# Block-causal attention and a SoLU layer on one core: squares to a scratch tile, spaced source rows, one copy for the second AV result, new planner constants

## The chip, the cores and the metric

The kernel runs on one core of a Trainium2 chip. A core has TensorE (PE, matmuls, with its weight loads shown apart as PEld), VectorE (DVE), ScalarE (ACT), GpSimd (POOL), SyncE (SP, which here issues the DMAs) and 16 DMA engines. The metric is device time in microseconds of one execution, lower is better. The kernel before took 726.27 us, the median of 3 runs (724.88 to 729.66).

## The reference

Attention over 8 batches of 8 heads, 576 positions, head width 64, in float32, with a causal mask in blocks of 64 positions, and then a layer on the 4608 tokens of width 512 with an inner width of 1024:

```python
scores = scale * np.matmul(q, k.transpose(0, 1, 3, 2))
mask = block_i >= block_j
scores = np.where(mask, scores, -1000000000.0)
scores = scores - np.max(scores, axis=-1, keepdims=True)
attn = np.exp(scores)
attn = attn / (np.sum(attn, axis=-1, keepdims=True) + 1e-09)
# np.matmul(attn, v), then heads side by side: x is [4608, 512]
h = x @ w_in                                   # w_in float64
e = np.exp(h - h.max(-1)); sm = e / (e.sum(-1) + 1e-9)
solu = h * sm
ln = (solu - mean) / np.sqrt(var + 1e-06) * g_ln
out = (ln @ w_out).astype(np.float32)
```

The weights come as float64; the kernel reads their 32-bit words and builds float32 values from them.

## The kernel before, in words

**Attention.** Two heads of a batch are one pair, 32 pairs in all. Queries are cut into units of 128 rows, `(h, i)` for head h and block i, 0 to 3; a unit needs 128·(i+1) keys. The last 64 queries of both heads form one unit, `LAST`. For each pair, PE makes the scores (L567, L573), DVE masks and takes the row maxima (L598, L602), ACT does the exponentials and their sums (L614), and the rows are divided by their sums on POOL, DVE or ACT (L632 to L634). The probabilities lie in `pb`, four rows of 25 slots of 32 columns in each partition; `soff` gives each unit's first slot. They must be transposed before the AV product. For the first eight entries (`PEP`, the four pairs of batch 0 in two parts each), PE transposes them (L554). For the other 28, DVE transposes blocks of 32 by 32 (L640), and four DMAs from SP (`place`, L648) carry 32 partitions of `pb` each to 128 partitions of `pt`. The AV product (L660) multiplies `pt` with the values in `vr` into two PSUM banks: `av0` takes the queries up to 384, `av1` the other 192 of each head. ACT or DVE copies both to the tile `xt` (`copy`, L412): `av0` in one piece, `av1` in three, since its two halves hold their columns in a different order.

**The layer.** A tile is 128 tokens, 36 in all, of three batches' `xt` in rotation. Matrices are split in a high and a low part, so each product is three matmuls. PE makes `h` (L746, two halves of 12 matmuls of 512 columns; the second product, L816, has as many), DVE takes the maximum (L752), ACT the exponential (L753), DVE the product (L754), POOL centres it (L761). ACT squares it and sums the squares (L764): only the sum `m[:, 4:5]` is used, the squared values go to the output tile `ob[i]`, `i = t % 2`, and are overwritten later. DVE transposes blocks (L782) and four DMAs move them (`ct` from `zb`, L786), the result is split (L794 to L798), PE makes the second product (L816), ACT or DVE writes it, scaled, to `ob[i]` (L820, L821), and SP stores it (L822). The first four tiles and the last use PE for the transpose (L804).

**The start.** The first batch's `q`, `k` and two blocks of `v` are fetched first (`fetch0`, L435, L438); then `prep` (L362 to L380) turns each of 8 blocks of `w_in` and 8 of `w_out` into high and low parts on ACT, POOL and DVE.

**The order of the work.** Nothing is ordered at run time. `Schedule.run` simulates the five engines when the kernel is built: each operation has a duration, a key, and perhaps alternatives on other engines; when an engine is free, it takes the ready operation with the smallest key, and the order found is written out. DMA operations carry `dma`, the time that they occupy the queue, and `tail`, the time from there to landing; SP is held back when the queue is more than `DEPTH` ahead. Keys are built from the dictionary `PARAMS`: attention's are the pair's number p plus a constant by kind (`s` scores, `se` maxima and exponentials, `sr` and `sp` division, `pt` transposes, `pe` placing, `av` and `ae` AV product and copies, `ld` and `lv` loads; an ending `32` for the first eight entries, `A` for the first part of batch 0), the layer's are `h0` (first four tiles: `hA`) plus `hs` per tile, and the weights' are `w0 + w1·n` for `w_in` and `w2 + w3·c` for `w_out`. Engines work through their queues in order.

The lines that write `ob` and place the probabilities:

```python
ACT.activation(ob[i].bitcast(mybir.dt.bfloat16), cz, AF.Square, accum_out=m[:, 4:5])   # L764
for a_ in (0, 2, 1, 3):                                                              # L647, L648
    SP.dma_start(pt_[:, a_].rearrange("p s i -> p (s i)"), pb[32 * a_ : 32 * a_ + 32].rearrange("p r s i -> p (r s i)"))
```

Of the kernel before, what the change touches and what calls it, by code (L numbers as in the profile page):

```python
# [31 lines left out]
NPT = 2  # L32
# [15 lines left out]
    "a_sp": 15.151, "a_sp32": 33.434, "a_lf": -19.843, "a_w": -53.076, "a_xh": 7.699, "a_xl": 42.171,  # L48
    "a_c": 45.045, "a_o": 1.147, "np": 32, "l0": 10.919, "a_cl": 82.304, "a_ai": -19.611, "aff": -198.558,
    "a_t3": -226.025, "a_cm": -13.873, "a_cg": -136.828, "a_sa": -14.146, "a_sa32": 226.312, "a_qh": -1.948,  # L50
    "a_kl": -33.0, "a_ch": 8.609, "a_chd": 185.089, "a_clo": -87.939, "ct0": -0.422, "qA": -20.741,
    "qeA": -57.386, "sA": -4.436, "seA": -5.607, "srA": 89.822, "spA": 243.774, "ptA": 46.328, "peA": -58.037,
    "avA": 18.17, "aeA": 50.13, "ldA": -276.676, "lvA": 10.694, "a_spA": -0.83, "a_saA": 1.199, "w2": 5.397,
    "w3": 49.83, "hA": 84.857,
# [7 lines left out]
class Schedule:  # L62
# [49 lines left out]
    def run(self):  # L112
# [20 lines left out]
        while events:  # L133
# [18 lines left out]
            for e in engs:  # L152
# [59 lines left out]
def kernel(  # L212
# [73 lines left out]
    ms = [sb(f"ms{i}", [8]) for i in range(2)]  # L286
# [22 lines left out]
    def PS(i):  # L309
        return pst[sc.slot[i]]  # L310
# [73 lines left out]
    n = 0  # L384
# [490 lines left out]
```

## Time and profile before

| | |
|---|---|
| time, median of 3 | 726.27 us (724.88 to 729.66) |
| profiled execution, its own time | 728.37 us |
| its span, first to last instruction | 726.6 us |
| mean granted TensorE clock | 0.974 |
| moved by DMA | 109.74 MB, mean 151 GB/s |

The page gives one profiled execution. An engine's busy time is a share of the span; "idle before" names the time an engine stood still just before a group of instructions, and what ended it. A line such as `PE ps L660 <- DMA pt<-pb: 4.1, 4, 1.2` says that PE stood before instructions of line 660 until a DMA from `pb` to `pt` landed, 4.1 us in total, 4 times, 1.2 us at most. In a table of stretches, each row has the stretch, its length, the busy time of each engine with its instructions, the granted clock of PE, the mean busy share of the DMA engines and the GB/s moved. A line of the timeline has start, duration, engine, line, operation and count, and in brackets the idle time before it with its cause.

### The profile page before, as it was taken

What the parts mean: (1) busy time and instruction counts of PE and PEld (TensorE: products, weight loads), DVE (VectorE), ACT (ScalarE), POOL (GpSimd) and SP (SyncE); (2) the same over time, 40 slices, a digit from 0 to 9 for tenths busy, and PEclk for the clock granted to TensorE, in tenths of its full rate; (3) what the DMA queues carried; (4) which work ended last, traced back from release to release, by engine and by line L of the source; (5) the groups of instructions that cost most, each with busy time, mean ns of one, the idle gap of its engine ahead of it and who ended that gap; (6) DMA issues with size and microseconds to landing.
All of it is one profiled execution on the core that took longest, in us unless ns stands there. A gap on an engine that the chain in (4) does not pass through costs nothing.

```text
span 726.6 us, 14364 instructions
## 1 busy us (share of the span) xinstructions
PE 673.5 (93%) x4747; PEld 530.2 (73%) x4747; DVE 574.3 (79%) x1252; ACT 499.8 (69%) x1286; POOL 359.6 (49%) x512
## 2 busy tenths in 40 slices
PE   5687897999999999989999999999989999999997
PEld 4565575777777777767777777777767777788885
DVE  2798989896999888978798979698878977455552
ACT  3686889686878867767786778587857885444432
POOL 1367566443665454546555554556456555223211
PEclk8598989999999999999999999999999999999999
DMA  9855358596969897969896989797969767322221
GB/s 172 195 96 130 99 114 141 123 130 169 165 170 174 213 176 194 155 166 172 203 172 163 176 205 158 173 187 180 179 160 188 171 167 168 105 72 72 73 73 44
DMA packets 223434, 109.74 MB, mean 151 GB/s; under 512 B 186496, under 2 KB 202368, under 8 KB 223360
## 3 DMA queue, kind: packets, MB, share of 16 engines
q1 hardware_dynamic: 222320, 108.56, 74.9%
q8 instruction: 37, 0.61, 0.4%
q10 hardware_dynamic: 1040, 0.26, 0.2%
q14 instruction: 37, 0.30, 0.1%
HBM read 37.23 MB, written 9.44 MB: 64 GB/s over the span
## 4 chain that ended last, share of the span: by engine, by line
PE 55%; DVE 12%; DMA 12%; ACT 9%; SPq 6%; issue 3%; POOL 2%; DVEq 0%; ACTq 0%; POOLq 0%
PE ps L816 20%; PE ps L746 16%; PE ps L660 9%; PE ps L573 6%; DMA pt<-pb 5%; ACT pb L614 3%; PE ps L567 3%; DVE nm L602 2%; DMA kz<-in_k_dram 2%; SPq L648 2%; DVE pb L640 2%; ACT pb L634 2%; DMA ct<-zb 2%; SPq L461 2%; DMA ub<-in_moe_w_in_dram 1%
## 5 line engine op out<-in xcount | busy, mean ns | idle before, releaser
L614 ACT ACTIVATE pb<-ps,nm 128x384 f32<-128x384 f32 (+4 forms) x288 | 157.1, 555 | 74.2 <-DVE nm L602 58.6
L602 DVE TENSOR_REDUCE nm<-ps 128x1 f32<-128x384 f32 (+4 forms) x288 | 132.1, 505 | 0.4
L640 DVE STREAM_TRANSPOSE pb<-pb 128x1536 f32<-128x1536 f32 (+1 forms) x56 | 101.6, 1829 | 11.4 <-ACT pb L634 7.8
L660 PE MATMUL ps<-pt,vr 128*64 128x128 f32 (+1 forms) x1648 | 92.6, 269 | 12.9 <-DMA ct<-zb 7.1
L660 PEld LDWEIGHTS ps<-pt,vr 128*64 128x64 f32 x1648 | 81.8, 137 | 30.8 <-issue 12.7
L634 ACT ACTIVATE pb<-pb,rz 128x512 f32<-128x512 f32 (+4 forms) x185 | 92.1, 566 | 17.4 <-DVE rz L625 14.5
L746 PE MATMUL ps<-wih,xh 128*128 128x512 f32 x288 | 84.3, 414 | 3.7 <-ACT pb L614 3.7
L798 POOL TENSOR_TENSOR cl<-ct,ch 128x512 fp32r<-128x512 f32 x40 | 51.6, 1293 | 71.0 <-ACT ch L794 69.0
L632 POOL TENSOR_SCALAR pb<-pb,rz 128x512 f32<-128x512 f32 (+4 forms) x101 | 63.9, 644 | 40.3 <-DVE rz L625 17.1
L816 PE MATMUL ps<-woh,ch 128*128 128x512 f32 x288 | 80.7, 402 | 0.0
L746 PE MATMUL ps<-wil,xh 128*128 128x512 f32 x288 | 79.5, 398 | 0.0
L816 PE MATMUL ps<-woh,cl 128*128 128x512 f32 x288 | 78.8, 395 | 0.0
L746 PE MATMUL ps<-wih,xl 128*128 128x512 f32 x288 | 78.7, 395 | 0.0
L816 PE MATMUL ps<-wol,ch 128*128 128x512 f32 x288 | 78.7, 395 | 0.0
L761 POOL TENSOR_SCALAR ub<-ub,ms 128x1024 f32<-128x1024 f32 x31 | 35.7, 1151 | 82.7 <-DVE ms L755 68.5
L573 PE MATMUL ps<-kh,qh 64*128 64x128 f32 (+3 forms) x256 | 58.3, 386 | 11.4 <-ACT pb L614 7.5
L746 PEld LDWEIGHTS ps<-wih,xh 128*128 128x128 f32 x288 | 50.9, 190 | 23.8 <-issue 8.6
L746 PEld LDWEIGHTS ps<-wil,xh 128*128 128x128 f32 x288 | 54.8, 190 | 13.0
L746 PEld LDWEIGHTS ps<-wih,xl 128*128 128x128 f32 x288 | 54.3, 189 | 13.1 <-POOL xl L725 0.3
L816 PEld LDWEIGHTS ps<-woh,cl 128*128 128x128 f32 x288 | 54.2, 188 | 12.8
L816 PEld LDWEIGHTS ps<-wol,ch 128*128 128x128 f32 x288 | 54.2, 188 | 12.8
L816 PEld LDWEIGHTS ps<-woh,ch 128*128 128x128 f32 x288 | 51.5, 188 | 11.4 <-ACT pb L614 0.4
(124 smaller groups left out, 1299.3 us busy)
## 6 DMA issues: line engine op xcount, KB each, us to landing
pt<-pb SPq DMA_DIRECT2D x112, 400.0 KB, 6.1
ct<-zb SPq DMA_DIRECT2D x124, 128.0 KB, 2.7
out_dram<-ob SPq DMA_DIRECT2D x36, 256.0 KB, 3.1
vr<-in_v_dram SPq DMA_DIRECT2D x64, 128.0 KB, 3.8
qz<-in_q_dram SPq DMA_DIRECT2D x56, 144.0 KB, 4.7
kz<-in_k_dram SPq DMA_DIRECT2D x56, 144.0 KB, 3.9
ub<-in_moe_w_in_dram SPq DMA_DIRECT2D x8, 512.0 KB, 6.6
ub<-in_moe_w_out_dram SPq DMA_DIRECT2D x16, 256.0 KB, 3.2
```

The lines of the kernel that those rows point to most:

```text
L567: PE.matmul(t[:, 192 + k0 : 192 + k1], w_, x_[:, k0:k1], start=n_ == 0, stop=n_ == 2)
L573: PE.matmul(PS(sps[h])[:, off : off + 128 * (i_ + 1)], w_[half[h], 128 * i_ : 128 * i_ + 128], x_[half[h], 0 : 128 * (i_ + 1)], start=n_ = ...
L602: op("DVE", t_dve(wid[u]), lambda sp=sp, off=off, u=u: DVE.tensor_reduce(out=nm_[u], in_=PS(sp)[:, off : off + wid[u]], axis=AX.X, op=ALU. ...
L614: ACT.activation(dst, src, AF.Exp, bias=nm_[u], accum_out=z_[zg][:, zc : zc + 1])
L632: op("POOL", 0.836 * nn + 243, lambda b=b, zg=zg, zc=zc: POOL.tensor_scalar(out=puv(pb, b, pep), in0=puv(pb, b, pep), scalar1=rz_[zg][:, z ...
L634: ("ACT", t_act(nn, 133), lambda b=b, zg=zg, zc=zc: ACT.activation(puv(pb, b, pep), puv(pb, b, pep), AF.Copy, scale=rz_[zg][:, zc : zc + 1 ...
L640: op("DVE", 1.058 * 128 * (s1 - s0) + 86, lambda s0=s0, s1=s1: DVE.transpose(pb[:, :, s0:s1, :], pb[:, :, s0:s1, :]), r=[("P", i, b) for b ...
L660: PE.matmul(dst(PS(av)[half[h]]), w_, pt_[:, a0:a1, sl, :], start=start, stop=stop)
L746: PE.matmul(o_, a_[:, c, :], w_[:, c, s_], start=(si == 0 and c == 0), stop=(si == 2 and c == NKI - 1))
L761: op("POOL", 1097, lambda: POOL.tensor_scalar(out=dst, in0=src, scalar1=m[:, 3:4], scalar2=1.0, op0=ALU.add, op1=ALU.mult), r=[uk, ("m3", ...
L798: alts=[("POOL", 1225, lambda c_=c_, h_=h_, l_=l_: POOL.tensor_tensor(out=l_, in0=c_, in1=h_.bitcast(F32), op=ALU.subtract), K["a_clo"])])
L816: PE.matmul(o_, a_[:, c, :], w_[:, c, :], start=(hf == 0 and si == 0 and c == 0), stop=(hf == 1 and si == 2 and c == 7))
```

## The change

Six things change.

- The squares of L764 go to a tile `junk` of 1024 bf16 values, used for nothing else.
- Each of the four rows of a partition of `pb` is followed by 8 floats that are not used, so that rows start 3232 bytes apart and not 3200. The placing DMAs read four separate runs per partition. For the first eight entries, whose `pb` is one flat run, the tile is used without gaps.
- In `pb`, `LAST` and unit (1, 3) change places, and the second AV product of head 1 writes its columns in the order of head 0. `av1` is then copied in one piece of 128 partitions and 192 columns.
- The planner's times of DMAs change (loads, placing, `ct` moves, stores: `tail` smaller, most `dma` larger; the load of `g_ln` now has one), some ACT durations grow by 44 to 100 ns, and the reciprocal of the sums counts as using the port shared with POOL.
- In the planner, a DMA holds back its issuing engine only if that is SP.
- All keys in `PARAMS` are new, chosen with noise on the planned times.

```diff
-    "nd": 2, "ld": -4.623, "lv": -205.654, "q": 664.814, "qe": 5.24, "s": 19.253, "se": 17.198, "sr": 87.69,
...
+    "nd": 2, "ld": 62.912, "lv": -14.91, "q": 350.247, "qe": -0.799, "s": -76.343, "se": 33.052,
...
-    w0 -17.548, w1 15.388, w2 5.397, w3 49.83, seA -5.607, hA 84.857, h0 -314.652, hs 70.244
+    w0 -280.763, w1 139.108, w2 -2.125, w3 2.401, seA -1274.541, hA 488.772, h0 189.244, hs 89.159
...
-                    engfree[e] = max(done, dmafree - DEPTH)
-                    done = max(engfree[e], dmafree)
+                    if e == "SP":
+                        engfree[e] = max(done, dmafree - DEPTH)
+                    done = max(done, dmafree)
...
-    soff = {(0, 0): 0, (0, 1): 1, (0, 2): 3, (1, 0): 6, (1, 1): 7, (1, 2): 9, (0, 3): 12, LAST: 16, (1, 3): 21}
+    soff = {(0, 0): 0, (0, 1): 1, (0, 2): 3, (1, 0): 6, (1, 1): 7, (1, 2): 9, (0, 3): 12, (1, 3): 16, LAST: 20}
...
-    pbs = [sb(f"pb{i}", [4, NSL, 32]) for i in range(2)]
+    PAD = 8
+    pbt = [sb(f"pb{i}", [4, NSL * 32 + PAD]) for i in range(2)]
+    pbs = [x[:, :, 0 : NSL * 32].rearrange("p r (s i) -> p r s i", i=32) for x in pbt]
+    pbf = [x.rearrange("p r n -> p (r n)")[:, 0 : NSL * P].rearrange("p (s k) -> p s k", k=P) for x in pbt]
...
+    junk = sb("junk", [DFF], mybir.dt.bfloat16)
...
-            op("SP", nd_ * 640, lambda: fetch(raws, src), w=[("ub", 0), ("ub", 1)], key=key, tail=2700, dma=2540)
+            op("SP", nd_ * 640, lambda: fetch(raws, src), w=[("ub", 0), ("ub", 1)], key=key, tail=1550, dma=3000)
...
-                op("SP", 3000, load2, w=[(nm, 0), (nm, 1)], key=lk, tail=2400, dma=4300)
+                op("SP", 2400, load2, w=[(nm, 0), (nm, 1)], key=lk, tail=1650, dma=4500)
...
-                    SP.dma_start(pt_[:, a_].rearrange("p s i -> p (s i)"), pb[32 * a_ : 32 * a_ + 32].rearrange("p r s i -> p (r s i)"))
-
-            op("SP", 4 * 600, place, r=tk, w=ptk, key=p + K["pe" + sfx], tail=3200, dma=6800)
+                    SP.dma_start(pt_[:, a_].rearrange("p s i -> p (s i)"), pbt[i][32 * a_ : 32 * a_ + 32, :, 0 : NSL * 32])
+
+            op("SP", 4 * 600, place, r=tk, w=ptk, key=p + K["pe" + sfx], tail=1950, dma=7900)
...
+            def flat2(c0):
+                return lambda t: t[:, c0 : c0 + 128].rearrange("p (s a i) -> p a s i", s=2, a=2)
...
-                        sl = slice(12 + j, 17 + j, 4) if h == 0 else slice(16 + j, 22 + j, 5)
-                        mm(av1, h, low(0), j, 2 * h, 2 * h + 2, sl, j == 0, False)
+                        mm(av1, h, low(0) if h == 0 else flat2(64), j, 2 * h, 2 * h + 2, slice(12 + 4 * h + j, 21 + j, 8 - 4 * h), j == 0, False)
                     else:
-                        mm(av1, h, flat(128 - 128 * h, 2), j, 2 * h, 2 * h + 2, 20, False, True)
+                        mm(av1, h, flat(128, 2), j, 2 * h, 2 * h + 2, 24, False, True)
...
-                    mm(av1, h, flat(64, 2), j, 2 - 2 * h, 4 - 2 * h, 12 + 9 * h + j, j == 0, j == 3)
+                    mm(av1, h, flat(64 - 64 * h, 2), j, 2 - 2 * h, 4 - 2 * h, 12 + 4 * h + j, j == 0, j == 3)
...
-        for av, rows, parts in ((av0, both, [first]), (av1, half[0], [(0, 384, 192)]), (av1, half[1], [(64, 384, 128), (0, 512, 64)])):
-            for c_, q_, l_ in parts if av else ():
+        for av, rows, (c_, q_, l_) in ((av0, both, first), (av1, both, (0, 384, 192))):
+            if av:
...
-        op("ACT", t_act(1024, 135), lambda: ACT.activation(ob[i].bitcast(mybir.dt.bfloat16), cz, AF.Square, accum_out=m[:, 4:5]), r=[ck], w=[("m4", i), ("ob", i)], key=key + K["sq"])
+        op("ACT", t_act(1024, 135), lambda: ACT.activation(junk, cz, AF.Square, accum_out=m[:, 4:5]), r=[ck], w=[("m4", i)], key=key + K["sq"])
...
-            op("SP", 4 * 600, move, r=["zb"], w=["ct"], key=key + K["ct"], tail=2800, dma=2500)
+            op("SP", 4 * 600, move, r=["zb"], w=["ct"], key=key + K["ct"], tail=2100, dma=1400)
```

The two lines with `w0` to `hs` gather entries of `PARAMS` that stand apart in the file.

More of the change, by code (lines that the diff above doesn't have):

```diff
@@ L41 @@
 PARAMS = {
[6 rows of a table removed]
[L48 to L54, printed above, removed]
[7 rows of a table added]
+    "a_xh": -17.362, "a_xl": 61.822, "a_c": -1.256, "a_o": -259.759, "np": 32, "l0": -0.452, "a_cl": 8.632,
+    "a_ai": 115.957, "aff": -59.213, "a_t3": -2.636, "a_cm": -260.295, "a_cg": 5.98, "a_sa": -49.519,
+    "a_sa32": 11.94, "a_qh": -143.616, "a_kl": -147.619, "a_ch": -110.329, "a_chd": 7.775, "a_clo": -70.343,
+    "ct0": 8.417, "qA": 26.653, "qeA": -1.392, "sA": 220.496, "seA": -1274.541, "srA": -11.458, "spA": -6.353,
+    "ptA": -4.82, "peA": 19.324, "avA": 168.423, "aeA": 41.283, "ldA": 248.31, "lvA": -67.979,
+    "a_spA": -161.148, "a_saA": -281.747, "w2": -2.125, "w3": 2.401, "hA": 488.772,
 }
@@ L359, in prep @@
             nd_, fetch = (2, heads) if gcol is None else (4, rows)
-            op("SP", nd_ * 640, lambda: fetch(raws, src), w=[("ub", 0), ("ub", 1)], key=key, tail=2700, dma=2540)
+            op("SP", nd_ * 640, lambda: fetch(raws, src), w=[("ub", 0), ("ub", 1)], key=key, tail=1550, dma=3000)
         high = raw[:, :, 1].bitcast(F32)
-        op("ACT", 520, lambda: ACT.activation(T3.bitcast(I32), raw[:, :, 0], AF.Copy, scale=2.0**-29), r=[kr_], w=[k3], key=key,
+        op("ACT", 570, lambda: ACT.activation(T3.bitcast(I32), raw[:, :, 0], AF.Copy, scale=2.0**-29), r=[kr_], w=[k3], key=key,
            alts=[("POOL", 640, lambda: POOL.tensor_scalar(out=T3.bitcast(I32), in0=raw[:, :, 0], scalar1=2.0**-29, scalar2=1.0, op0=ALU.mult, op1=ALU.mult), K["a_t3"])])
@@ L381, in prep @@
         wkeys.append((name, "l"))
-    op("SP", 4 * 500, lambda: rows(gt, g_ln.rearrange("(c r j) -> r j c", r=4, j=32)), w=["gt"], key=K["w2"], tail=2100)
+    op("SP", 4 * 500, lambda: rows(gt, g_ln.rearrange("(c r j) -> r j c", r=4, j=32)), w=["gt"], key=K["w2"], tail=2100, dma=2800)
     n = 0
@@ L410, in copy @@
     def copy(which, n_, aps, scale, w, key, ps, r=()):
-        op("ACT", t_act(n_), lambda: ACT.activation(aps()[0], aps()[1], AF.Copy, scale=scale), r=r, w=w, key=key, ps=ps,
+        op("ACT", t_act(n_, 100 if n_ < 200 else 0), lambda: ACT.activation(aps()[0], aps()[1], AF.Copy, scale=scale), r=r, w=w, key=key, ps=ps,
            alts=[("DVE", t_dve(n_), lambda: DVE.tensor_scalar(out=aps()[0], in0=aps()[1], scalar1=scale, scalar2=None, op0=ALU.mult), K[f"e{which}"])])
-    def flat(pb):
-        return pb.rearrange("p r c i -> p (r c i)").rearrange("p (s k) -> p s k", k=P)
     def puv(pb, u, pep):
         if pep:
-            return flat(pb)[:, soff[u] : soff[u] + u[1] + 1, :]
+            return pb[:, soff[u] : soff[u] + u[1] + 1, :]
         return pb[:, :, soff[u] : soff[u] + u[1] + 1, :]
@@ L532, in attention @@
             op("DVE", t_dve(S) + 30, lambda z=z: DVE.transpose(z, z), r=[zk], w=[zk], key=kk)
-            op("ACT", t_act(S), lambda z=z, hi=hi, scale=scale: ACT.activation(hi, z, AF.Copy, scale=scale), r=[zk], w=[(x + "h", iq)], key=ke,
+            op("ACT", t_act(S, 44), lambda z=z, hi=hi, scale=scale: ACT.activation(hi, z, AF.Copy, scale=scale), r=[zk], w=[(x + "h", iq)], key=ke,
                alts=[("POOL", 0.836 * S + 243, lambda z=z, hi=hi, scale=scale: POOL.tensor_scalar(out=hi, in0=z, scalar1=scale, scalar2=1.0, op0=ALU.mult, op1=ALU.mult), K["a_qh"])])
@@ L553, in trans @@
                 for s_ in range(c0, c1):
-                    PE.transpose(PS(pt)[:, (s_ - c0) * P : (s_ - c0 + 1) * P], flat(pb)[:, s_, :], ident)
+                    PE.transpose(PS(pt)[:, (s_ - c0) * P : (s_ - c0 + 1) * P], pb[:, s_, :], ident)
             op("PE", 109 * (c1 - c0), trans, r=[(x, i, b) for b in bs for x in ("P", "P2")], w=[("pt2", p % NPT, s_) for s_ in range(c0, c1)] + [("flat", i, c0)], key=p + K["pt" + sfx], opens=pt)
@@ L627, in attention @@
                 zk = [("z", i, u) for u in bs]
-                op("DVE", 300, recip, r=zk, w=[("rz", i, zg)] + zk, key=p + K["sr" + sfx])
+                op("DVE", 300, recip, r=zk, w=[("rz", i, zg)] + zk, key=p + K["sr" + sfx], port=True)
                 for b in bs:
```

13 lines of the change are left out of this document (7 added, 6 removed), and 11 rows, old and new, of the table PARAMS.

## The prediction

> **What bounds the kernel now.** I read the first part of the page for the engine that carries the work, the windows by stage for where that engine is idle, and then the list of what TensorE (PE) waited for in each stage.
>
> ```profile
> span 726.6 us, 14364 instructions
> PE 673.5 (93%) x4747; PEld 530.2 (73%) x4747; DVE 574.3 (79%) x1252; ACT 499.8 (69%) x1286; POOL 359.6 (49%) x512
> ```
>
> ```profile
> core 0: us, PE busy (x) PEld busy (x) DVE busy (x) ACT busy (x) POOL busy (x), PEclk, DMA share, GB/s
> 0.00:130.00 130.00, 99.28 (x830) 78.56 (x831) 105.15 (x253) 95.03 (x252) 71.57 (x101) 0.86 0.64 132
> 130.00:610.00 480.00, 462.15 (x3367) 361.00 (x3367) 409.01 (x900) 358.94 (x953) 261.21 (x377) 1.00 0.90 174
> 610.00:726.60 116.60, 112.11 (x556) 90.64 (x552) 60.18 (x101) 45.83 (x82) 26.78 (x35) 1.00 0.29 79
> 150.00:600.00 450.00, 432.52 (x3137) 338.29 (x3136) 384.48 (x839) 339.69 (x901) 245.97 (x354) 1.00 0.92 176
> ```
>
> PE is the bound: 673.5 of 726.6 us busy. Its idle time is 130.00 − 99.28 = 30.7 us in the start, 480.00 − 462.15 = 17.9 us in the middle, 116.60 − 112.11 = 4.5 us at the end, 53.1 us in all. Nothing in the change takes a matmul away, so the floor is about 673.5 us, less what the start loses to its clock (0.86 against 1.00). The end is almost pure second-layer matmuls plus a drain, and has nothing to give. DMA is the second pressure: its engines are 0.92 busy in the middle. These are the middle's PE waits, all of them:
>
> ```profile
> PE ps L660 <- DMA ct<-zb: 7.1, 4, 2.6
> PE ps L660 <- DMA pt<-pb: 4.1, 4, 1.2
> PE ps L573 <- ACT pb L614: 3.5, 7, 1.5
> PE ps L573 <- ACT xt L412: 1.2, 2, 0.8
> PE ps L567 <- DVE ub L754: 1.2, 1, 1.2
> PE ps L804 <- POOL zb L761: 0.3, 1, 0.3
> ```
>
> They sum to 17.4 us of the 17.9. L660, the AV product, reads `pt` and not `ct`: the two first rows are both waits for the placing transfers to land, with a `ct` move in the same queue landing last. So 11.2 us of the middle is eight AV products that stood too early in PE's order, and 4.7 us is ACT being late.
>
> **The change part by part.** *The second AV result in one copy.* The matmuls stay as many and as wide; only their columns in the bank move, so PE's work changes by nothing. The copies are these:
>
> ```profile
> L412 ACT ACTIVATE xt<-ps 64x192 f32<-64x192 f32 x32 | 10.2, 318 | 2.5 <-PE ps L660 2.4
> ...
> L412 ACT ACTIVATE xt<-ps 64x128 f32<-64x128 f32 x32 | 8.7, 272 | 0.4
> ...
> L412 ACT ACTIVATE xt<-ps 64x64 f32<-64x64 f32 x32 | 6.6, 208 | 0.0
> ```
>
> Before, each pair pays 318 + 272 + 208 = 798 ns; after, one copy of 192 columns, 318 ns by the first row (the time follows the columns there). That is 0.48 us a pair, 32 × 0.48 = 15.4 us of ACT, and the bank and the `xt` columns are free 0.48 us sooner. ACT is not the bound, so only the waits on ACT are credited: the two waits on `xt` lose 0.48 each (1.0 us), and of the seven waits on the exponentials (L614), 7 × 0.48 = 3.4 us if such copies stood in front of every one, I take half, 1.7. Together −2.6 us, between 0 and −4.3.
>
> *Squares to their own tile.* The squares (L764) wrote their unused result into the output tile `ob` and so had to wait for the store of two tiles earlier.
>
> ```profile
> ACT ob L764 <- DMA out_dram<-ob: 26.8, 14, 5.3
> ```
>
> ```profile
> ACT ob L764 <- DMA out_dram<-ob: 9.2, 6, 2.4
> ```
>
> ```profile
> ACT ob L764 <- DMA out_dram<-ob: 17.6, 8, 5.3
> ```
>
> The first row is the wait in the whole span, the second the middle, the third from 610 us on. The instruction is as long as before. Of the 26.8 us of ACT idle time, 17.6 lie in the end, where PE is full, and 9.2 in the middle, where the PE waits on ACT are the 4.7 us that the copies have drawn on already. I cost it at nothing beyond them; the bound is the rest, 4.7 − 2.6 = −2.1. The wait itself passes to the copy of the final product (L820), which writes `ob` later in the same tile, after 24 further matmuls; if that cover were gone, L820 would stand up to 5.3 us, with the exponentials queued behind it on ACT.
>
> *Source rows 32 bytes apart.* Four transfers per pair take 32 partitions of `pb` and spread them over 128 partitions of `pt`. The four rows of a partition no longer join into one run.
>
> ```profile
> DMA packets 223434, 109.74 MB, mean 151 GB/s; under 512 B 186496, under 2 KB 202368, under 8 KB 223360
> ```
>
> ```profile
> L648 SPq DMA_DIRECT2D pt<-pb x112: 542/1154/3262, 117.9 to 615.3; - x112
> ...
> DMA to landing us min/median/max: 4.8/6.1/8.8
> ```
>
> Between 2 and 8 KB there are 223360 − 202368 = 20992 packets; 112 × 128 = 14336 of them are the placing's destination rows of 3200 bytes, so the trace already counts runs of the size that the padded source has. Number, size, partitions and issuing queue stay. I take 0, since the packets are the same; the bounds are the ends of the landing row applied to the eight late AV products: 8 × (4.8 − 6.1) = −10.4 us, 8 × (8.8 − 6.1) = +21.6 us. A longer issue on SP (the row's 542 to 3262 ns is mostly waiting for room) would hold up the loads, `ct` moves and stores queued behind it, and lies inside that. The transposes of `pb` (L640) walk four separate runs per partition before and after; I cost the wider step at nothing, since DVE is 409 of 480 us busy in the middle and PE shows no wait on it there but one of 1.2.
>
> The Trainium skill ("DMA: Bandwidth & Descriptors", section "How a descriptor splits into AXI transactions") speaks against this edit: a run that doesn't start on a 256-byte boundary fetches from the boundary below. From an aligned base, rows 3232 bytes apart would take 100 + 105 + 102 + 107 = 414 beats of 32 bytes where one joined run takes 400, an estimate of 3.5%, which would make the sum some 1.7 us longer. No row here shows it.
>
> *Fitted times and new keys.* Durations, landing times and keys change no instruction, only the order on each queue, and every queue is reordered. Three edits to the planner have one answer: a DMA holding only SP back changes nothing, since every planned DMA stands under SP; `port` on the reciprocal and the added ACT overheads move operations by fractions of a microsecond. What the order is worth is bounded by the waits that order makes.
>
> ```profile
> 309.13 3.29 DMA ct<-zb
> 312.46 2.98 PE ps L660 x52
> 316.43 2.80 PE ps L816 x12
> ```
>
> This is one of the eight late AV products on the chain: it stands 52 matmuls long, and a block of 12 ready matmuls (2.80 us) follows soon after. One such block put ahead of the product covers every one of the eight waits (longest 2.6). So another order can win between 0 and 11.2 us; the planner's placing and `ct` times, landing sooner in one term and occupying longer in another, don't say on which side its new order falls, and I take half, −5.6.
>
> In the start the order matters more:
>
> ```profile
> PE ps L554 <- ACT pb L634: 10.2, 2, 9.3
> ```
>
> ```profile
> 16.22 0.68 ACT L362 ACTIVATE ob<-ub 128x512 int32<-128x512 uint32 x1 [3.62 <-DMA ub<-in_moe_w_in_dram]
> ...
> 16.79 0.48 ACT L614 ACTIVATE pb<-ps,nm 128x256 f32<-128x256 f32 x1
> ...
> 22.85 0.47 PE L554 MATMUL ps<-ident,pb 128*128 128x128 f32 x1 [9.29 <-ACT pb L634]
> ```
>
> ```profile
> 10.00:22.80 12.80, 1.84 (x24) 0.65 0.95 171
> 22.80:38.00 15.20, 13.62 (x102) 0.51 0.76 165
> ```
>
> ACT stood 3.62 us at the first weight conversion (L362), whose load had not landed, with exponentials of the first pairs (L614) queued behind it, and PE then idled 9.29 us. The new keys put the first pairs' exponentials (`seA`, −1274.5) far ahead of that conversion (`w0`, −280.8), where −5.6 and −17.5 stood close. If they go first, the gap loses the 3.62 us, at most 3.62 + 0.57 (the conversion itself). I take −3.6. PE's clock after the gap is 0.51 for 13.62 us of work; the gap stays about 5.7 us, so I leave the clock as it is; if it were full there, 13.62 × 0.49 = 6.7 us more would go.
>
> The Trainium skill ("TensorE: Matmul & The Clock Gate", "Part 1: The HAM clock gate") has PE's clock halved after an idle window of about 3.4 us and restored after as long a busy stretch. The 0.51 behind a gap of 9.29 us agrees; by it the 6.7 us would go only if the gap fell under 3.4 us.
>
> Against this stand the weights: the second half of `w_in` gets keys up to −280.8 + 7 × 139.1 = 693, behind all of `w_out` (at most −2.1 + 7 × 2.4 = 14.7), where before both ran side by side.
>
> ```profile
> 60.00:80.00 20.00, 3.23 (x12) 2.10 (x12) 0.88 0.50 103
> 80.00:100.00 20.00, 3.05 (x12) 2.18 (x12) 0.91 0.41 124
> 100.00:120.00 20.00, 7.65 (x24) 5.56 (x24) 0.91 0.71 88
> ```
>
> These are the first layer's matmuls (L746) alone: 13.9 us of them fill PE before 120 us. Delayed weights would cost between nothing (attention fills in) and 13.9 us. I take 0.
>
> Sum: −2.6 − 0 − 0 − 5.6 − 3.6 = −11.8 us, a span of 714.8. The profiled execution took 728.37 us, 1.8 above its span and 0.3% above the median of 726.27. So 716.6 us on its scale, and 716.6 × 726.27 / 728.37 = 714.5 as a median: 715 us, 1.6% faster.
>
> **The rivals.** *The waits only move.* The eight late products are eight among 28 pairs; another order makes others late, because DMA at 0.92 leaves no room. Then only the copies count: 726.3 − 2.6 = 723.7 us. For it: DMA stays as full, and the old order had few waits per pair already. Against: a single block would cover each.
>
> *The weights come late (slower).* PE's filler before 120 us is missing: 726.3 + 13.9 − 2.6 = 737.6 us, with the start's gain lost too. It decides, against the copies' relief and the measuring limit, once some 10 us of the 13.9 find no attention matmuls in their place. For it: the keys. Against: attention's matmuls take PE at any time in the start, and conversions run whenever nothing more urgent is ready.
>
> *The padding makes placing slower.* At 0.92 the DMA engines have 450 × 0.08 = 36 us to spare between 150 and 600 us, over some 26 placings: 1.4 us each. Beyond that they become the bound; at 2.0 us more per placing (inside the landing row) it is 26 × 2.0 − 36 = +16, 742 us. For it: four times as many source runs. Against: the packets.
>
> *The padding does nothing*, in either direction, is part of my forecast.
>
> **How the numbers follow.** Chances: forecast 0.55; moved waits 0.28; late weights 0.11; slower placing 0.06. About 1% (719 to 733.5) is what a measurement of this kernel can tell from no change. Faster 0.55, same 0.28, slower 0.17. The low end takes the copies' −4.3, the squares' −2.1, all 11.2 and the start's 4.2, with a little of the clock's 6.7: about −24, 702 us. The high end reaches past the moved waits to the nearer part of the late weights, 735. Outside lie the slower placing, half of the late weights and a few in a hundred below.
>
> **What would show it.** Copies: L412 with 128x192, about 318 ns, and ACT some 15 us less busy. Squares: no wait of L764 on the store, and none in its place at L820. Padding: the placing's landing median within 0.5 us of 6.1. Order: PE's waits of L660 on DMA under 6 us in the middle. Start: PE's gap near 13 to 23 us under 6 us, and L746 before 120 us. The forecast is wrong if PE's idle time stays above 50 us, or if the middle's DMA share reaches 1.

## The result, and the profile after

The kernel after takes 716.69 us, the median of 4 runs (715.26 to 718.76), where the kernel before took 727.49 in 4 runs. The ratio is 0.9855, with a 95% interval of 0.9811 to 0.990. Here and below, an execution more than 1.5% above the fastest of its kernel is left out of medians and ratios; there are two such, both with the edits alone. The profiled execution took 716.22 us. The lines of the code have moved by a few: scores are L570 and L576 now, exponentials L617, placing L651, AV product L663, copies L417 (ACT) and L418 (DVE), first layer product L751, squares L769, second product L821.

The first part of the page after, and the table of the same three stages as before:

```profile
span 714.3 us, 14282 instructions
PE 673.9 (94%) x4747; PEld 530.8 (74%) x4747; DVE 593.2 (83%) x1353; ACT 453.7 (64%) x1136; POOL 353.3 (49%) x497
```

```profile
0.00:130.00 130.00, 107.45 (x877) 85.63 (x879) 106.83 (x267) 103.19 (x260) 68.65 (x103) 0.86 0.63 132
130.00:610.00 480.00, 466.18 (x3402) 364.37 (x3399) 432.62 (x988) 314.95 (x817) 261.54 (x363) 1.00 0.90 177
610.00:714.30 104.30, 100.29 (x474) 80.83 (x472) 53.77 (x99) 35.58 (x60) 23.08 (x31) 0.99 0.25 72
```

PE's busy time has stayed (673.9 against 673.5), with the same matmuls. Its idle time fell from 30.7 to 22.5 us in the start, from 17.9 to 13.8 in the middle and from 4.5 to 4.0 at the end: 12.7 us less, against a span that is 12.3 us shorter. So in these two traces two thirds of the gain lie in the start, of which the last section has more to say. What PE still waits for in the middle, without two rows of 0.3 us:

```profile
PE ps L821 <- ACT pb L617: 8.6, 7, 2.8
PE ps L751 <- DVE ub L759: 2.6, 2, 2.1
PE ps L576 <- ACT pb L617: 1.1, 2, 0.8
PE ps L821 <- DVE cl L813: 0.6, 1, 0.6
```

The waits of the AV product on the placing transfers, 11.2 us before, are gone. A row that was not there before stands at the head: the second product of the layer (L821) waits for exponentials. It doesn't read them. It needs a PSUM bank, and that bank still holds scores. One such place on the timeline, at 442 to 446 us:

```profile
442.13 1.44 DVE L535 STREAM_TRANSPOSE qz<-qz 128x576 f32<-128x576 f32 x2 [2.78 <-DMA qz<-in_q_dram]
...
444.87 1.32 DVE L605 TENSOR_REDUCE nm<-ps 128x1 f32<-128x256 f32 x3
...
445.30 0.47 ACT L617 ACTIVATE pb<-ps,nm 128x256 f32<-128x256 f32 x1 [2.98 <-DVE nm L605]
...
446.01 1.56 PE L821 MATMUL ps<-woh,ch 128*128 128x512 f32 x4 [1.89 <-ACT pb L617]
```

DVE stood 2.78 us for a load of queries. The row maxima were queued behind it, ACT stood 2.98 us for them, and PE stood 1.89 us for the bank that ACT's exponential then released. Over the whole span, DVE stood 17.2 us for such loads (the second row below), against 2.1 before (the first row, of the kernel before). This wait and that of L821 go together in the traces of the same order: without the spacing of the rows (below) they are 20.0 and 10.9 us, with three copies 11.3 and 4.3.

```profile
DVE qz L532 <- DMA qz<-in_q_dram: 2.1, 5, 1.0
```

```profile
DVE qz L535 <- DMA qz<-in_q_dram: 17.2, 9, 3.4
```

The merged copies, in the view that keeps shapes apart, and the placing DMAs with their landing:

```profile
L418 DVE TENSOR_SCALAR xt<-ps 128x192 f32<-128x192 f32 x26 | 8.8, 339 | 1.4 <-PE ps L663 1.3
```

```profile
L417 ACT ACTIVATE xt<-ps 128x192 f32<-128x192 f32 x6 | 2.0, 339 | 1.9 <-PE ps L663 1.7
```

```profile
L651 SPq DMA_DIRECT2D pt<-pb x112: 542/1000/3263, 117.0 to 606.5; - x112
...
DMA to landing us min/median/max: 4.9/6.1/8.5
```

The new order gives 26 of the 32 merged copies to DVE and only 6 to ACT; one takes 339 ns on either. Landing is as before (6.1 us). ACT's longest waits at the squares name their inputs now and none names a store, where before 26.8 us of them were for the store of the output tile:

```profile
ACT junk L769 <- DVE ub L767: 21.0, 9, 2.5
ACT junk L769 <- POOL ub L766: 19.3, 18, 2.2
```

In the start, ACT still stands at the first weight conversion (L367), longer than before if anything (3.70 against 3.62 us). PE's gap is shorter all the same, 5.81 us where it was 9.29:

```profile
14.85 0.66 ACT L367 ACTIVATE ob<-ub 128x512 int32<-128x512 uint32 x1 [3.70 <-DMA ub<-in_moe_w_in_dram]
15.41 0.46 ACT L617 ACTIVATE pb<-ps,nm 128x256 f32<-128x256 f32 x1
...
16.36 0.58 PE L576 MATMUL ps<-kh,qh 64*128 64x256 f32 x2 [5.81 <-ACT pb L617]
```

### The profile page after: what moved, and what is told of

It is laid out like the page before. It is cut to its first block, busy times and chain, and to the rows that moved or that the text cites. A ratio compares the mean times of both kernels' runs of the same rounds, so it can differ in the third digit from the quotient of the medians.

```text
span 714.3 us, 14282 instructions
## 1 busy us (share of the span) xinstructions
PE 673.9 (94%) x4747; PEld 530.8 (74%) x4747; DVE 593.2 (83%) x1353; ACT 453.7 (64%) x1136; POOL 353.3 (49%) x497
## 4 chain that ended last, share of the span: by engine, by line
PE 29%; DVE 23%; DMA 6%; ACT 5%; issue 5%; SPq 4%; POOL 1%; DVEq 0%; POOLq 0%; ACTq 0%
PE ps L821 12%; PE ps L751 11%; DVE pb L643 6%; DMA qz<-in_q_dram 5%; DVE nm L605 5%; SPq L464 4%; PE ps L663 3%; DVE ms L757 2%; DVE ub L759 2%; PE ps L576 2%; ACT pb L637 2%; ACT pb L617 2%; DVE zb L787 1%; DVE qz L535 1%; ACT ub L758 1%
## 5 line engine op out<-in xcount | busy, mean ns | idle before, releaser
L617 ACT ACTIVATE pb<-ps,nm 128x256 f32<-128x256 f32 (+4 forms) x288 | 157.2, 554 | 103.0 <-DVE nm L605 69.7
L605 DVE TENSOR_REDUCE nm<-ps 128x1 f32<-128x256 f32 (+4 forms) x288 | 132.6, 507 | 0.2
L663 PEld LDWEIGHTS ps<-pt,vr 128*64 128x64 f32 x1648 | 82.5, 140 | 19.0 <-issue 4.6
L663 PE MATMUL ps<-pt,vr 128*64 128x128 f32 (+1 forms) x1648 | 94.8, 273 | 0.1
L821 PE MATMUL ps<-woh,ch 128*128 128x512 f32 x288 | 81.7, 405 | 9.8 <-ACT pb L617 8.6
L751 PE MATMUL ps<-wih,xh 128*128 128x512 f32 x288 | 82.8, 409 | 4.6 <-DVE ub L759 2.6
L637 ACT ACTIVATE pb<-pb,rz 128x128 f32<-128x128 f32 (+4 forms) x166 | 84.8, 573 | 2.9 <-DVE rz L628 2.8
L803 POOL TENSOR_TENSOR cl<-ct,ch 128x512 fp32r<-128x512 f32 x52 | 66.6, 1289 | 33.9 <-ACT ch L799 30.0
L821 PE MATMUL ps<-wol,ch 128*128 128x512 f32 x288 | 79.5, 398 | 0.0
L821 PE MATMUL ps<-woh,cl 128*128 128x512 f32 x288 | 79.0, 396 | 0.0
L751 PE MATMUL ps<-wil,xh 128*128 128x512 f32 x288 | 78.8, 395 | 0.0
L751 PE MATMUL ps<-wih,xl 128*128 128x512 f32 x288 | 78.6, 394 | 0.0
L821 PEld LDWEIGHTS ps<-woh,ch 128*128 128x128 f32 x288 | 51.4, 189 | 25.2 <-POOL qdh L546 9.0
L751 PEld LDWEIGHTS ps<-wih,xh 128*128 128x128 f32 x288 | 50.9, 188 | 24.7 <-issue 8.4
L576 PE MATMUL ps<-kh,qh 64*128 64x128 f32 (+3 forms) x256 | 57.5, 385 | 9.5 <-ACT pb L617 7.9
L821 PEld LDWEIGHTS ps<-wol,ch 128*128 128x128 f32 x288 | 54.8, 190 | 12.9
L821 PEld LDWEIGHTS ps<-woh,cl 128*128 128x128 f32 x288 | 54.7, 190 | 12.9
L751 PEld LDWEIGHTS ps<-wih,xl 128*128 128x128 f32 x288 | 54.1, 188 | 12.9
L751 PEld LDWEIGHTS ps<-wil,xh 128*128 128x128 f32 x288 | 54.2, 188 | 12.8
L769 ACT ACTIVATE junk<-ub 128x1024 bf16<-128x1024 f32 x31 | 32.8, 1057 | 42.6 <-DVE ub L767 21.0
L758 ACT ACTIVATE ub<-ps,ms 128x1024 f32<-128x1024 f32 x36 | 40.0, 1111 | 29.2 <-DVE ms L757 29.2
```

The source lines that it names most:

```text
L576: PE.matmul(PS(sps[h])[:, off : off + 128 * (i_ + 1)], w_[half[h], 128 * i_ : 128 * i_ + 128], x_[half[h], 0 : 128 * (i_ + 1)], start=n_ = ...
L605: op("DVE", t_dve(wid[u]), lambda sp=sp, off=off, u=u: DVE.tensor_reduce(out=nm_[u], in_=PS(sp)[:, off : off + wid[u]], axis=AX.X, op=ALU. ...
L617: ACT.activation(dst, src, AF.Exp, bias=nm_[u], accum_out=z_[zg][:, zc : zc + 1])
L637: ("ACT", t_act(nn, 133), lambda b=b, zg=zg, zc=zc: ACT.activation(puv(pb, b, pep), puv(pb, b, pep), AF.Copy, scale=rz_[zg][:, zc : zc + 1 ...
L663: PE.matmul(dst(PS(av)[half[h]]), w_, pt_[:, a0:a1, sl, :], start=start, stop=stop)
L751: PE.matmul(o_, a_[:, c, :], w_[:, c, s_], start=(si == 0 and c == 0), stop=(si == 2 and c == NKI - 1))
```

## The experiments

All medians below are of 6 to 12 runs. Where a diff stands for several lines of code, it is abridged. The kernel before was run beside them on the same chips and stood at 727.0 to 728.3 us.

**The order alone.** The queues of the kernel after in the same order, and the three edits of the code undone:

```diff
-    PAD = 8
+    PAD = 0
-    ACT.activation(junk, cz, AF.Square, accum_out=m[:, 4:5])
+    ACT.activation(ob[i].bitcast(mybir.dt.bfloat16), cz, AF.Square, accum_out=m[:, 4:5])
-    copy of av1: 128 partitions x 192 columns
+    copies of av1 at the same place: 64x192, 64x128, 64x64
```

In this order some tiles issue their squares ahead of the store of two tiles earlier, which uses the same `ob`; those stores carry squares, so that part of the output isn't the layer's. The work and its waits are.

> The changed kernel with its order of work on every queue kept, and its three edits of the program undone: no gap between source rows, squares back in the output tile (so they wait for the store again), the second AV result copied in three pieces. Theory A (the order carries the gain; copies are worth 2.6 us, squares and padding nothing): ratio to the kernel before about 0.989, some 719 us, with PE's start and its waits on the placing as in the changed kernel. Rival B (the edits carry the gain by relieving ACT, the order is only another order): ratio 0.997 or more, 725 us or more.

It took 725.3 us (721.74 to 729.12), a ratio of 0.9973 (0.9943 to 1.0003), as rival B had it. The longest of PE's waits in the middle, and ACT's wait for the stores over the whole span:

```profile
PE ps L824 <- ACT pb L617: 6.3, 6, 2.6
PE ps L576 <- DVE xt L711: 4.5, 10, 0.6
```

```profile
ACT ob L772 <- DMA out_dram<-ob: 34.6, 10, 5.7
```

(L824 is the second product here, L711 the copies on DVE.) The order does remove the waits on placing by itself, and brings the new ones by itself. It is worth about 2 us alone, far from 9, and its interval just reaches one. The three copies, on DVE now, are waited for at ten places, and ACT stands 34.6 us for stores.

**The edits alone.** The order of the kernel before, with the spaced rows, the tile `junk` and the single copy:

```diff
+    PAD = 8; junk = sb("junk", [DFF], mybir.dt.bfloat16)
-    soff = {..., LAST: 16, (1, 3): 21}          copies of av1: 64x192, 64x128, 64x64
+    soff = {..., (1, 3): 16, LAST: 20}          copy of av1: 128x192
```

> The kernel before with its order kept, and the three edits put in: padded source rows, squares in a tile of their own, the second AV result copied once, at the place of the first of the three old copies. Theory A: only the copies count, 724 us, ratio 0.996, and PE's 11.2 us of waits for the placing in the middle stay. Rival B: 718 us or less, ratio 0.988 or less.

It took 721.0 us (716.58 to 725.01), 0.9913 (0.9879 to 0.9947), between the two expectations. The waits of the AV product are all there, and the middle as a whole is no shorter:

```profile
PE ps L661 <- DMA pt<-pb: 8.6, 6, 2.6
PE ps L661 <- DMA ct<-zb: 4.1, 3, 1.4
```

```profile
130.00:610.00 480.00, 462.34 (x3360) 362.68 (x3360) 406.08 (x897) 348.57 (x904) 260.99 (x375) 1.00 0.89 176
```

So the edits, not the order, carry the larger share when each stands alone: about 6 us against about 2. Both together bring 10.8 us by the medians: with the edits in place the order brings 721.0 − 716.69 = 4.3, and with the order in place the edits bring 725.3 − 716.69 = 8.6. That is some 2 us more than the sum of both, which the intervals don't tell from nothing. Where the 6 us of the edits sit isn't shown. PE idles 480.00 − 462.34 = 17.7 us in the middle, as in the kernel before; the trace is shorter in the start, by 2.9 us of idle time, and by 3.4 us of PE's busy time (670.1 against 673.5).

**The edits one by one, in the old order.** The squares:

```diff
-    ACT.activation(ob[i].bitcast(mybir.dt.bfloat16), cz, AF.Square, accum_out=m[:, 4:5])
+    ACT.activation(junk, cz, AF.Square, accum_out=m[:, 4:5])
```

> The kernel before with its order kept and one edit: the squares go to a tile of their own. The three edits together gave ratio 0.9913 in the old order, 6 us, more than the copies' 2.6 by the prediction. Theory A (squares are worth nothing, since PE is full where ACT waits for the store): ratio 0.999 to 1.001. Rival B (the squares' wait held ACT and through it PE; it is the larger part of the 6 us): ratio 0.995 or less.

724.51 us (720.18 to 726.76), 0.9951 (0.9927 to 0.9975), at the edge of rival B. The single copy, with `soff` and the AV columns as in the change, and nothing else:

```diff
-    soff = {..., LAST: 16, (1, 3): 21}          copies of av1: 64x192, 64x128, 64x64
+    soff = {..., (1, 3): 16, LAST: 20}          copy of av1: 128x192
```

> The kernel before with its order kept and one edit: the second AV result copied once (with the slots and columns moved for it), no padding, squares in the output tile. Theory A (the copies are what the edits gain): ratio 0.991 to 0.996. Rival B (they gain nothing, ACT being off the path): ratio 0.998 or more.

726.0 us (721.89 to 728.59), 0.9976 (0.995 to 1.0001), between the two. And the kernel before, with no edit at all, as a measure of what one more execution shows:

> The kernel before, unchanged: a second profile of it, for what differs between two executions of one kernel in the start, where the first weight block landed at 16.2 us in one profile and at 14.2 to 15.7 us in others. Theory A: ratio 1.000, and its start within 1 us of the first profile at 130 us of the span. Rival B (the start varies by itself): by 130 us its matmuls stand 2 us or more away from the first profile's.

727.24 us (723.4 to 732.93), 0.9995 (0.9969 to 1.0022), with 2.3 us more of PE's idle time in its start than the first trace (33.0 against 30.7), as rival B had it. The squares are worth some 3 us, with an interval clear of one. The copy is worth 1 to 2 us by the medians, with an interval that just reaches one; ACT is 499.8 − 486.6 = 13.2 us less busy by it:

```profile
PE 675.5 (93%) x4747; PEld 532.0 (73%) x4747; DVE 575.0 (79%) x1252; ACT 486.6 (67%) x1222; POOL 360.5 (50%) x512
```

Where the squares' gain sits is only partly seen. In the middle PE idles 480.00 − 463.44 = 16.6 us with them, against 17.9 and 17.6 in the two traces of the kernel before, so about 1 us is there:

```profile
130.00:610.00 480.00, 463.44 (x3401) 363.95 (x3396) 406.00 (x903) 361.15 (x956) 262.68 (x376) 0.99 0.89 175
```

```profile
PE ps L660 <- DMA pt<-pb: 8.0, 4, 2.7
PE ps L660 <- DMA ct<-zb: 4.4, 3, 2.1
...
PE ps L660 <- ACT pb L634: 1.0, 1, 1.0
PE ps L573 <- ACT xt L412: 0.8, 1, 0.8
PE ps L573 <- ACT pb L614: 0.5, 1, 0.5
```

The waits of the scores (L573) on ACT fall from 4.7 to 1.3 us. Those of the AV product on placing grow from 11.2 to 12.4 us, and one of 1.0 us on the division (L634) is new.

Another part shows in the start, where it can't belong: PE idles 29.8 us there against 30.7 and 33.0, and the first squares run at 126 us. That is how executions differ (last section), and where the other two microseconds of the medians come from stays open.

**The spacing of the rows.** The kernel after with `PAD` at nothing and the four rows read as one run again, the order kept:

```diff
-    PAD = 8
+    PAD = 0
-    SP.dma_start(..., pbt[i][32 * a_ : 32 * a_ + 32, :, 0 : NSL * 32])
+    SP.dma_start(..., pbt[i][32 * a_ : 32 * a_ + 32].rearrange("p r n -> p (r n)"))
```

> The changed kernel without the 8 floats between source rows, everything else and every queue's order the same. Theory A (the padding does nothing): landing median of the placing 6.1 us, ratio 0.9855 as with the padding, within 0.3%. Rival B (it speeds the placing): landing 6.5 us or more and 3 us or more longer. Rival C (it slows the placing): shorter by 2 us or more.

718.09 us (716.49 to 720.41), 0.9877 (0.9841 to 0.9914), against 0.9855 (0.9811 to 0.990) with the spacing. The landing:

```profile
DMA to landing us min/median/max: 5.1/6.2/8.3
```

Landing differs by 0.1 us in the median. The intervals lie over each other for most of their length: a gain of 1.4 us isn't shown, nor a loss.

**Three copies in the new order.** Each of the 32 merged copies of the kernel after is three again, on the engine that had it; spacing and `junk` stay.

```diff
-    one op: xt[128 partitions, 192 columns] <- av1
+    one op of three instructions, on the same engine at the same place: 64x192, 64x128, 64x64
```

> The changed kernel with every queue's order kept and the second AV result copied in three pieces, on the engine that its order gives (DVE for 26 of 32, ACT for 6). Theory A (the copies count by how long the score banks stay taken): some 4 us longer than the changed kernel, ratio about 0.992, with PE's waits on the copies, which took 4.5 us in the order run alone, back in the middle. Rival B (squares carry the difference between the order alone and the changed kernel): ratio 0.988 or less.

719.77 us (717.51 to 720.74), 0.9893 (0.9868 to 0.9917), between the two expectations. By the medians about 3 us are the copy's in the new order, where 26 of the copies stand on DVE, the busier engine there; the intervals of the two kernels overlap. The wait on the copies, the second row of the order alone, is seen here as well:

```profile
PE ps L824 <- ACT pb L617: 4.3, 2, 2.2
PE ps L576 <- DVE xt L711: 4.1, 10, 0.5
```

```profile
130.00:610.00 480.00, 466.11 (x3400) 363.68 (x3399) 442.55 (x1030) 318.35 (x831) 261.86 (x362) 1.00 0.89 176
```

But it comes in place of another: the second product's wait on the exponentials is 4.3 us here and 8.6 in the kernel after, and PE idles 13.9 us in the middle here and 13.8 there. So the single copy does take that wait away, and the trace doesn't show that this is what the 3 us are. The order alone (725.3) has the squares in `ob` and no spacing besides; these two are together 5.5 us.

**The stall in the start.** The kernel after with one instruction moved: on ACT, the first conversion of weights (L367) goes behind the four exponentials that stood behind it.

```diff
-    L367 conversion (waits for w_in) ; L617 x4
+    L617 x4 ; L367 conversion (waits for w_in)
```

> The changed kernel with one instruction moved on one queue: the first weight conversion on ACT stands behind the four exponentials of the first two score tiles, which in the changed kernel wait behind it while its load lands (ACT idle 3.70 us, PE then idle 5.81 us). Theory A (that wait in ACT's queue is what holds PE in the start): PE's gap falls from 5.8 to about 2 us, the span shortens by about 3.7 us, ratio about 0.980; if PE's clock also stays up, more. Rival B (the start is held by the weights' conversions, which now come later): the gap goes but comes back before 60 us, span unchanged within 1 us or longer.

719.07 us (713.82 to 723.17), 0.9883 (0.9837 to 0.9929): no gain, as rival B had it. The timeline of PE and ACT in it:

```profile
12.91 0.62 PE L576 MATMUL ps<-kh,qh 64*128 64x256 f32 x2 [1.91 <-ACT pb L617]
...
15.73 0.67 ACT L367 ACTIVATE ob<-ub 128x512 int32<-128x512 uint32 x1 [2.07 <-DMA ub<-in_moe_w_in_dram]
...
17.07 0.89 ACT L637 ACTIVATE pb<-pb,rz 128x256 f32<-128x256 f32 x2
...
17.61 0.29 PEld L557 LDWEIGHTS ps<-ident,pb 128*128 128x128 f32 x2 [2.92 <-ACT pb L637]
17.61 0.69 PE L557 MATMUL ps<-ident,pb 128*128 128x128 f32 x2 [2.63 <-DVE zb L374]
```

The gap falls from 5.81 to 1.91 us, and the next wait takes what was won: the transposes (L557) stand 2.63 us. They read `pb`, of which ACT divides a part (L637), and that division still stands behind the conversion in ACT's queue, as the row of their weight loads (PEld) has it; the DVE instruction that the matmuls' own row names doesn't write `pb`. Moving the division ahead as well wasn't tried.

**Loads that the order takes to land later.** The chain at 446 us began with a load that came later than the order had room for. The planner of the kernel after takes the loads of queries and keys to land 1.65 us behind the time that they occupy the queue. Three orders were written out with 1.0 us more, each with its own set of keys, and one order with the old figure and other keys as a control. The code of the computation is that of the kernel after in all four.

```diff
-                op("SP", 2400, load2, w=[(nm, 0), (nm, 1)], key=lk, tail=1650, dma=4500)
+                op("SP", 2400, load2, w=[(nm, 0), (nm, 1)], key=lk, tail=2650, dma=4500)
     (and all keys in PARAMS chosen again)
```

> The kernel after, whose order is written out anew with one time of the planner changed: the loads of queries and keys are taken to land 1.0 us later (2.65 instead of 1.65 us behind the issue), and the priorities are chosen again for that. All code of the computation is the kernel's after. Theory: in the kernel after, VectorE stands 17.2 us (9 times) for loads of queries, its row maxima and then ScalarE's exponentials come late behind that, and TensorE waits 8.6 us ahead of the second product (L821) for the score bank that these exponentials still hold. Then here VectorE's wait for the query loads falls below 6 us, TensorE's wait of L821 on the exponentials below 3 us, TensorE's idle time between 130 and 610 us from 13.8 to below 9, and the time to about 712 (ratio to before 0.979). Rival: every order leaves about 12 to 15 us of such waits in the middle, since something else is late whenever one wait goes; then VectorE's wait for the loads falls as well, but TensorE's idle time in the middle stays between 11 and 16 us with other rows at its head, and the time stays between 715 and 720 (0.983 to 0.990).

> As late_loads_1, with another set of priorities chosen for the same later landing, so that what follows does not rest on one order. Theory: VectorE's wait for the query loads below 6 us, TensorE's wait of L821 on the exponentials below 3 us, its idle time in the middle below 9 us, time about 713 (ratio 0.980). Rival: VectorE's wait for the loads falls, TensorE's idle time in the middle stays at 11 to 16 us, time 715 to 721 (0.983 to 0.991).

> A third order in which the loads of queries and keys are taken to land 1.0 us later (2.65 us behind the issue), from other priorities than late_loads_1 (median 703.8 us, TensorE idle 7.8 us between 130 and 610 us) and late_loads_2 (714.2 us, 16.9 us). All code of the computation is the kernel's after. Theory: the later landing is what brings the time down, and late_loads_2 is the exception; then VectorE's wait for the query loads is below 3 us, TensorE's idle time in the middle at most 11 us, and the time 703 to 710. Rival: the later landing only takes this wait away, and where the others fall is chance of the order; then VectorE's wait is below 3 us as well, but TensorE idles 12 to 18 us in the middle and the time is 712 to 719.

> Another order for the kernel after, with the loads of queries and keys left at their landing 1.65 us behind the issue, and priorities chosen again, from a start far from the kernel's own. All code of the computation is the kernel's after. In the kernel after, VectorE's wait for the query loads is 17.2 us and TensorE's wait of L821 on the exponentials 8.6 us; in late_loads_1 and late_loads_2, whose orders take these loads 1.0 us later, they are 0.2 and 0.2 us, and at most 1.4 us. Theory: the early landing in the planner makes these waits, in every order made with it; then VectorE's wait for the query loads is again above 10 us here, and TensorE idles 13 us or more between 130 and 610 us. Rival: the waits belong to the one order of the kernel after; then VectorE's wait is below 5 us here too. The time by both is about 715 to 728, since the planner's own account of this order is worse than that of the kernel after: the waits decide, not the time.

| order | median us | ratio (95%) | DVE's wait for queries | PE idle 0 to 130 us | PE idle 130 to 610 us |
|---|---|---|---|---|---|
| kernel after | 716.69 | 0.9855 (0.9811 to 0.990) | 17.2 | 22.5 | 13.8 |
| late_loads_1 | 703.8 | 0.9686 (0.965 to 0.9722) | 0.2 | 23.9 | 7.8 |
| late_loads_2 | 714.22 | 0.9828 (0.9786 to 0.9869) | 0.2 | 24.1 | 16.9 |
| late_loads_3 | 711.38 | 0.977 (0.9727 to 0.9814) | 3.6 | 23.9 | 11.7 |
| early_loads | 727.85 | 1.0007 (0.9976 to 1.0037) | 0.6 | 31.5 | 12.8 |

The stretch from 130 to 610 us of late_loads_1, and its three longest rows of PE waits there:

```profile
130.00:610.00 480.00, 472.22 (x3476) 373.26 (x3472) 450.54 (x1033) 320.09 (x836) 234.80 (x328) 1.00 0.88 180
```

```profile
PE ps L576 <- ACT xt L417: 1.8, 3, 0.7
PE ps L576 <- ACT pb L617: 1.6, 2, 1.2
PE ps L663 <- DMA pt<-pb: 1.4, 1, 1.4
```

late_loads_1 is the fastest kernel here: 3.1% under the kernel before and, by intervals that lie apart, under the kernel after. The wait of L821 on the exponentials is gone in it, as the theory had it. Of the 12.7 us of span that separate it from the kernel after (714.3 − 701.6), 6.0 are idle time of the middle and 8.1 are PE's busy time (673.9 to 665.9), less 1.4 more idle time elsewhere. Of the busy time a part may go with the mean granted clock, 0.976 against 0.970: 673.9 × 0.006 / 0.976 = 4.1 us, an estimate. But late_loads_2 has the same 0.976 and 671.5 us of busy time, only 2.4 less than the kernel after. So most of the 8.1 us isn't explained.

Yet the theory that I put to the test doesn't hold as it stood. The control keeps the early landing and has almost no wait for queries either, so the wait belongs to the one order of the kernel after and doesn't come with the planner's figure in every order. And late_loads_2 loses that wait just as fully and idles 3 us more in the middle, with other rows in its place. late_loads_3 meets neither of its expectations: its wait of 3.6 us is above what both had, and its idle time and its median lie between theirs. The three late orders came out at 703.8, 711.4 and 714.2, all at or under the kernel after. That the later landing is the reason is not shown: the control was also the worst of the four by the planner's own account, so its 727.85 us may have that cause. And it doesn't lose its time where these waits are. Its middle idles less than that of the kernel after; of the 10.8 us that its trace is longer (725.1 − 714.3), 9.0 are idle time ahead of 130 us (31.5 − 22.5).

## Why the prediction was right, and where it was not

The total was right: 715 forecast, 716.69 measured. The parts were not, and they were wrong in opposite directions: the order was priced too high and the edits too low by about as much. So the agreement of the total is in good part luck.

*The order, forecast −9.2 us (−5.6 in the middle and −3.6 in the start).* This is the term that was mis-sized. Alone it is worth about 2 us, on top of the edits 4. In the middle its first half came true to the letter: every wait of the AV product on placing is gone, all 11.2 us and not the half that I took. What failed is that I left nothing for what comes next. The rival "the waits only move" had that: 8.6 us came back at L821 and 2.6 at L751, and the idle time fell by 4.0 us, in the order alone by 17.9 − 15.4 = 2.5. For the order it had nothing where I had 9.2, and 2 to 4 were measured; but its 723.7 for the whole was too long, since its count of the edits was too small.

*The start, forecast −3.6 us from a stall that goes.* The step failed. The conversion still stands ahead of four exponentials and waits 3.70 us. I read the keys as the order, but a key decides only among operations that are ready: by the planner's own account the load has landed, and ACT is free, before the row maxima are done, and so the conversion goes first whatever its key. The number for PE's gap, under 6 us, came out (5.81) for another reason: ACT's wait for the load ended 1.4 us earlier in this execution, and PE has other matmuls (L576, not L557) behind the gap. That is luck: the order alone, with the same queues, has 6.19 us. The experiment that does make the stall go shows that taking the exponentials out of it was worth nothing, since the division behind them waits for the same load. The whole start nevertheless gained 8.2 us of idle time, more than I gave it. With the edits alone it had gained 30.7 − 27.8 = 2.9 and with the order alone 4.2, where two executions of the kernel before differ by 2.3 us already.

*The squares, forecast 0 with a bound of −2.1.* Mis-sized: some 3 us in the old order, 1.8 to 5.3 by the interval. So the zero is refuted, and the bound only by the median. I had let the copies use up those waits of PE that name ACT; with the squares alone they fall from 4.7 to 1.3 us, of which about 1 us is left as idle time saved, because others grow. Another path would be ACT's 9.2 us in the middle making the division (L634), the transposes and the placing late. The trace doesn't bear it out: the waits on placing are 12.4 us without ACT's wait and 11.2 with it. What the rest of the 3 us is stays open.

*The copies, forecast −2.6 between 0 and −4.3.* Right by the medians: 1 to 2 us in the old order, about 3 in the new, neither clear of its uncertainty. The relief of ACT was 13.2 us by itself (15.4 forecast), in part since one copy takes 339 ns and not 318. In the kernel after ACT is 46 us less busy. The 26 merged copies that the new order gives to DVE are another 8.8 us of that, and the rest is other work that it gives to other engines: of the splits of `ct` (L794, L799 now), ACT has 34 where it had 62.

*The spacing, forecast 0.* Right: landing 6.1 us with it, 6.2 without, and no time that can be told from none. The rule of the Trainium skill that spoke against it ("DMA: Bandwidth & Descriptors", section "How a descriptor splits into AXI transactions") would have had it 1.7 us dearer, an estimate. The measured difference is 1.4 us the other way, inside the uncertainty, so the rule is neither borne out nor refuted at this size.

*The weights, forecast 0.* Right: the first layer's matmuls fill PE before 120 us with 6.11 + 6.08 + 6.16 = 18.4 us, more than the 13.9 before, as these rows of the line L751 have it:

```profile
60.00:80.00 20.00, 6.11 (x24) 4.35 (x24) 0.98 0.46 104
80.00:100.00 20.00, 6.08 (x24) 4.36 (x24) 0.96 0.44 131
100.00:120.00 20.00, 6.16 (x25) 4.75 (x26) 0.78 0.67 84
```

*The clock, left at 0.51 behind the gap of 9.29 us.* I read it as the gap's work, and the trace of the kernel before shows otherwise. PE's last matmul ahead of the gap ends at 13.56 us, and the clock falls in this half microsecond and is 0.50 from 14.00 on (PE's busy time, its matmuls, the clock, DMA share and GB/s):

```profile
13.50:14.00 0.50, 0.06 (x1) 0.79 1.28 98
```

So a shorter gap need not have brought back the 6.7 us that I named beside the sum.

*The floor, 673.5 us of PE's busy time less what the clock takes in the start.* late_loads_1 has 665.9 with the same matmuls, and its clock in the start is 0.87 where it was 0.86. So the floor is less firm than I took it.

*The signs that I named.* The squares, the landing, the waits of L663 and the number of the gap came as written, the copies with 339 ns for 318 and 46 us of relief for 15. PE's idle time is 40.4 us, under the 50 that would have made the forecast wrong. Nearly all of them agreed while the split behind them was off. Signs that tell whether a step took place don't tell what it was worth.

## What to carry to other kernels

In this kernel, whose bounding engine is 93% busy, an order that cleared a wait was worth what stayed free after the next wait in line: price the second-latest input before crediting the first, and don't price an order by the waits that it clears. A scratch output that shares a tile with a store was worth a tile of its own (some 3 us), though the bounding engine's waits seemed to leave it nothing. And orders made with the same code spread over 3% (703.8 to 727.85 us), which is more than all edits of code here: measure several orders before judging an edit by one.

## What was not expected of the hardware

The load of the first weights ends ACT's wait at 16.22 us in one execution of the kernel before (the row is in the prediction) and at 15.46 in another of the very same program:

```profile
15.46 0.69 ACT L362 ACTIVATE ob<-ub 128x512 int32<-128x512 uint32 x1 [3.04 <-DMA ub<-in_moe_w_in_dram]
```

Nor does the granted clock come back at one time. Up to 126 us the squares alone issue the same instructions as the kernel before, and still its clock is at 0.79 between 28 and 36 us where the kernel before is at 0.50 (the first row is the kernel before, the second the squares alone):

```profile
28.00:36.00 8.00, 7.34 (x56) 6.11 (x54) 5.51 (x15) 6.07 (x22) 4.59 (x5) 0.50 0.73 167
```

```profile
28.00:36.00 8.00, 6.55 (x73) 5.89 (x73) 6.04 (x17) 5.56 (x22) 3.96 (x4) 0.79 0.68 152
```

In 8 us the one got through 56 matmuls, the other through 73, and the second execution of the kernel before through 34. A difference of two or three microseconds between the starts of two traces therefore says nothing of an edit.

The clock also falls without a long gap. With the exponentials first, PE's longest stand ahead of 14.5 us is 1.91 us, and the clock is at half from about then to 32 us (PE's busy time, its matmuls, clock, DMA share and GB/s):

```profile
12.00:16.00 4.00, 1.59 (x13) 0.80 1.16 174
16.00:20.00 4.00, 1.31 (x5) 0.50 0.24 19
20.00:24.00 4.00, 3.70 (x26) 0.50 0.91 225
```

Nor do 3.70 busy microseconds of 4 bring it back. The Trainium skill ("TensorE: Matmul & The Clock Gate", "Part 1: The HAM clock gate") has the clock halved after an idle window of about 3.4 us and restored after about 3.4 us of sustained activity. By it, the prediction had 6.7 us more to win once the gap fell under 3.4 us. The gap fell to 1.91 and 2.63 us here, and the clock did not stay up. It was lost behind a stretch that was thinly filled and not empty: from 11.0 to 14.4 us PE is busy for 1.15 us of 3.4, and from 14.5 on the clock is 0.50. In this case's traces the measurement goes against the rule as I used it.
